# Turning K in place on VectorE instead of through TensorE, in a one-core decode attention kernel

## The chip, the cores and the metric

The kernel runs on one core of a Trainium2 chip. The metric is the device time of one execution in microseconds, as a median of runs. A profile is one further execution, recorded instruction by instruction.

## The reference

One decoding step for 8 batches: layer norm of `x`, attention over the last W = 2048 keys of a cache, and a gated unit that multiplies the attention's output.

```
xn = layernorm(x)                                   # x: (8, 1, 512)
q  = (xn @ wq)  as 32 query heads of 128            # wq: 512 x 4096
k, v = last 2048 keys of k_cache, v_cache           # (8, 8 heads, 8192, 128), bf16; 4 query heads share one
o  = softmax(q k^T / sqrt(128)) v
s  = o @ wo                                         # wo: 4096 x 512
g  = silu((sigmoid(xn @ w_gate) * (xn @ w_up)) @ w_down)   # 512 -> 1792 -> 512
out = x + s * g
```

The inputs that must be read are 33.6 MB of K, 33.6 MB of V, 4.2 MB each of `wq` and `wo`, and 5.5 MB of the gated unit's weights, 81.0 MB in all.

## The kernel before

**Loads.** All big inputs pass through one ring of 9 SBUF buffers of 16 KB per partition (`RING`), 2 MB for a K or V load. SyncE's queue (SP) issues them in one fixed order, `issue_loads`: the two halves of `wq` (`wq_sb`), then K and V loads merged by slot (K load i at slot 4i, V load i at slot 4i + `PV_LAG`, here 11), with the three matrices of the gated unit (`wg_sb`, `wu_sb`, `wd_sb`) ahead of the last two V loads, and `wo` in eight pieces at the end. There are 16 K loads and 16 V loads. A load is issued when its turn has come and a buffer is free; a K buffer is free after its last slot, a V buffer likewise. A K or V load holds one batch and 4 of the 8 KV heads: 128 partitions are 32 groups of keys times 4 heads (head innermost), each with 64 keys in a row, 16 KB that lie together in HBM.

**Slots.** A K load is worked off in 4 slots, so there are 64 slots; `manual_schedule` keeps the written order on each engine. In slot t the loop calls `k_half(t, 0)` and `k_half(t, 1)`: 4 TensorE transposes each (L415) of 128 x 128 32-bit words (two bf16 of the head dimension are one word) into the PSUM tile `kT_ps`, and a VectorE copy (L419) into `kT_sb` that also sorts the columns by head. Every second slot `qk` does 8 score matmuls of 512 columns (L434) into `s_ps`; their four 32-column groups of the array are the four heads of the load, and successive matmuls go to different groups.

**Softmax.** One batch at a time, over 8 slots: the maximum on VectorE (`soft_max_part`, L446), a small fp32 matmul that joins the maxima (`soft_exp`, L455), Exp on ScalarE (L460), a VectorE 32 x 32 block transpose of the probabilities (`soft_turn`, L474), one matmul with a permutation (`soft_permute`, L480), a ScalarE copy (L488), and four VectorE products with a head mask (`soft_mask`, L496). The denominators are L507, L518 and L520.

**Values and the end.** `pv(u)`, 11 slots behind, does 8 matmuls of 256 columns (L536) per slot on four column groups; after four slots ScalarE copies `acc_ps` out (L549) and `pv_sum` sums it (L557, L564). The gated unit (L307 to L344) runs once, eight slots before the end of `pv`, and waits for its weights. After the last V load come `pv`, `pv_sum`, `o_rows` (L579, L588), then 64 matmuls with `wo` (L647), two VectorE products (L658, L660) and the store of the output.

Of the kernel before, what the change touches and what calls it, by code (L numbers as in the profile page):

```python
# [10 lines left out]
def kernel(  # L11
# [14 lines left out]
    P = 128  # L26
# [13 lines left out]

    GL = 4
# [5 lines left out]
    HALF = CC // 2  # L47
    NX = NG * NJ
    XR = NX * rep
    NT = B * NG  # L50
    SPB = NG * NJ
    NSLOT = B * SPB
    PV_LAG = SPB + 3

    D2 = Dh // 2
    NJ2 = NJ // 2
    QB = 2 * rep
    QPAD = XR - QB
    RING = 9
# [15 lines left out]
    ktpool = ctx.enter_context(tc.tile_pool(name="ktpool", bufs=2))  # L75
    ppool = ctx.enter_context(tc.tile_pool(name="ppool", bufs=2))
    psum = ctx.enter_context(
# [31 lines left out]
    def load_kv(cache, i, name):  # L109
        b, gg = divmod(i, NG)  # L110
        t = ring_tile([P, CH, Dh], name)
        load(
            t[:].rearrange("p c d -> p (c d)"),
            cache[b, GL * gg : GL * (gg + 1), win0:Sk, :].rearrange(
                "j (p c) d -> p j (c d)", c=CH
            ),
        )
        return t
# [26 lines left out]
    loads += [(3, 0), (3, 1)]  # L145
    loads_done = [0]
    free_bufs = [RING - 2]
# [15 lines left out]
    def issue_loads():  # L163
        while loads_done[0] < len(loads) and free_bufs[0] > 0:
            kind, i = loads[loads_done[0]]
            if kind == 0:
                k_tiles[i] = load_kv(A_k_cache, i, "k_sb")
            elif kind == 1:
                v_tiles[i] = load_kv(A_v_cache, i, "v_sb")
            elif kind == 2:  # L170
                load_mlp(i)
            else:
                load_wo(i)
            loads_done[0] += 1
            free_bufs[0] -= 1
# [10 lines left out]

    ident = consts.tile([P, P], bf16, name="ident")
    make_identity(nc, ident[:])
    identf = consts.tile([P, P], f32, name="identf")
    make_identity(nc, identf[:])  # L190
    SumM = consts.tile([P, P], f32, name="SumM")
    nc.gpsimd.memset(SumM[:], 0.0)
    for off in range(-rep * (NJ - 1), rep * NJ, rep):
        nc.gpsimd.affine_select(  # L194
            out=SumM[:],
            in_=SumM[:],
            compare_op=ALU.not_equal,
            fill=1.0,
            base=-off,
            pattern=[[-1, P]],  # L200
            channel_multiplier=1,
        )
    BS = rep * NJ
    SumM_blk = SumM[:].rearrange("p (a i) -> p a i", i=BS)
    nc.gpsimd.affine_select(
        out=SumM_blk,
        in_=SumM_blk,
        compare_op=ALU.is_ge,
        fill=0.0,
        base=0,  # L210
        pattern=[[-BS, P // BS], [0, BS]],
        channel_multiplier=1,
    )
    nc.gpsimd.affine_select(
        out=SumM_blk,
        in_=SumM_blk,
        compare_op=ALU.is_ge,
        fill=0.0,
        base=BS - 1,
        pattern=[[BS, P // BS], [0, BS]],  # L220
        channel_multiplier=-1,
    )
# [3 lines left out]
    Jneg = consts.tile([P, NJ], f32, name="Jneg")  # L226
    nc.vector.tensor_reduce(
        out=Jneg[:],
        in_=ident[:].rearrange("p (a j r) -> p j a r", j=NJ, r=rep),
        axis=AX.XY,  # L230
        op=ALU.add,
    )
    nc.vector.tensor_scalar(
        out=Jneg[:], in0=Jneg[:], scalar1=-scale, scalar2=None, op0=ALU.mult
    )

# [6 lines left out]
    )  # L243

# [6 lines left out]
    )  # L251

    perm = consts.tile([P, P], bf16, name="perm")
    nc.vector.tensor_copy(
        out=perm[:].rearrange("k (p gl) -> k p gl", gl=GL),
        in_=ident[:].rearrange("k (gl p) -> k p gl", gl=GL),
    )

    QW = 3 * QPAD + 2 * QB
    qz_sb = work.tile([P, B, Hkv, QW], bf16, name="qz_sb")
# [25 lines left out]
    xnT_ps = psum1.tile([P, KT, B], bf16, name="xnT_ps", tag="pT_ps")  # L288
# [14 lines left out]
    def unit_in(w_sb):  # L303
        d_ps = psum.tile([P, FQ], f32, name="d_ps", tag="kT_ps")
# [43 lines left out]
    def q_projection():  # L348
        HH = Hq // 2
        q_ps = [  # L350
            psum.tile([P, HH, 32], f32, name=f"q_ps{hh}", tag="kT_ps") for hh in range(2)
        ]
        for kt in range(KT):
            for hh in range(2):
                for c in range(4):
                    nc.tensor.matmul(  # L356
                        q_ps[hh][32 * c : 32 * (c + 1), :, :],
                        lhsT=xnT_sb[:, kt, :],
                        rhs=wq_sb[kt // KH][:, kt % KH, :].rearrange(
                            "p (h a m e) -> p h a m e", a=2, m=32, e=2  # L360
                        )[:, HH * hh : HH * (hh + 1), c % 2, :, c // 2],
                        start=(kt == 0),
                        stop=(kt == KT - 1),
                        tile_position=(0, 32 * c),
                        skip_group_check=True,
                    )
        for hh in range(2):
            q_sb = ppool.tile([P, HH * 32], bf16, name="q_sb", tag="p_bf")
            nc.scalar.copy(out=q_sb[:], in_=q_ps[hh][:].rearrange("p h m -> p (h m)"))
            qT_sb = ppool.tile([P, HH * 32], bf16, name="qT_sb", tag="pt_bf")  # L370
            nc.vector.transpose(out=qT_sb[:], in_=q_sb[:])  # L371
            GH = Hkv // 2
            for e in range(2):
                for c2 in range(2):
                    for r in range(rep):
                        nc.vector.tensor_copy(  # L376
                            out=qz_sb[
# [24 lines left out]

    CP = CC // 2
    HP = CP // 2

    def k_half(t, h2):
# [287 lines left out]
```

## Time and profile before

| | |
|---|---|
| median of 3 runs | 199.43 us (199.40 to 199.49) |
| profiled execution: time, span | 199.47 us, 197.7 us |
| mean granted TensorE clock | 0.904 |
| PE, DVE, ACT, POOL busy | 146.0, 125.2, 22.9, 9.0 us |
| read from HBM | 81.02 MB, 410 GB/s over the span |

The span runs from the first to the last instruction; the profiled execution's own time is 1.8 us longer. PE is TensorE's matmuls, PEld its weight loads, DVE is VectorE, ACT is ScalarE, POOL is GpSimd, SPq is SyncE's queue that issues loads. A group of instructions is told by its line (L419), and its columns are the busy time in all, the mean duration of one in ns, and the idle time just before them with what ended it.

### The profile page before, as it was taken

Reading aid. Unit: us, or ns where it says so; the run is one execution under the profiler, and the core shown is the slowest. Engines: PE = TensorE matmul, PEld = TensorE weight load, DVE = VectorE, ACT = ScalarE, POOL = GpSimd, SP = SyncE. Lnnn points to the kernel's source line nnn. Section 1 sums busy time; section 2 is a strip of 40 time slices with the busy share of each in tenths; the row PEclk is TensorE's granted clock in tenths of the full one; section 3 lists DMA queues with packets and bytes.
Section 4 is the critical chain, followed back from the end, with each engine's and each line's share of the span. In section 5 each row is a group of like instructions: output and inputs, shape, how many; then the busy total and the mean of one; then the engine's idle time right before and its main releaser. Section 6 shows DMA issues by size and latency. Waiting matters only on the chain.

```text
span 197.7 us, 3707 instructions
## 1 busy us (share of the span) xinstructions
PE 146.0 (74%) x1576; PEld 101.4 (51%) x1576; DVE 125.2 (63%) x280; ACT 22.9 (12%) x48; POOL 9.0 (5%) x22
## 2 busy tenths in 40 slices
PE   0073598939996997998697969686929697747693
PEld 0023455626765675665565756465626565325582
DVE  2809877964787887868765777577807786143111
ACT  2001000130011003002100110030000300600000
POOL 7910000000000000000000000000000000000000
PEclk9999999995999999999979699999975999697558
DMA  6999999999999999999999999999999999999980
GB/s 220 423 434 444 434 434 416 428 428 434 431 434 431 424 431 424 424 434 434 434 428 423 431 424 434 434 431 428 428 424 434 424 442 423 434 426 409 419 324 21
DMA packets 6864, 81.26 MB, mean 411 GB/s; under 512 B 792, under 2 KB 1088, under 8 KB 2112
## 3 DMA queue, kind: packets, MB, share of 16 engines
q1 hardware_dynamic: 6752, 81.01, 96.5%
q8 instruction: 12, 0.20, 0.4%
q14 instruction: 4, 0.03, 0.0%
q10 hardware_dynamic: 32, 0.01, 0.0%
q0 software_dynamic: 64, 0.01, 0.0%
HBM read 81.02 MB, written 0.01 MB: 410 GB/s over the span
## 4 chain that ended last, share of the span: by engine, by line
DMA 53%; PE 33%; DVE 10%; ACT 2%; issue 1%; SPq 0%; ACTq 0%
DMA k_sb<-in_A_k_cache_dram 32%; PE kT_ps L415 17%; DMA v_sb<-in_A_v_cache_dram 15%; DMA wq_sb<-in_A_wq_dram 6%; PE s_ps L434 5%; PE acc_ps L536 4%; DVE kT_sb L419 4%; PE a_ps L647 3%; DVE qz_sb L376 2%; DVE pT_sb L496 1%; PE oT_ps L557 1%; PE q_ps L356 1%; DVE qT_sb L371 1%; DVE pt_bf L474 1%; ACT L460 1%
## 5 line engine op out<-in xcount | busy, mean ns | idle before, releaser
L419 DVE COPY kT_sb<-kT_ps 128x512 f32<-128x512 f32 x128 | 83.7, 686 | 34.0 <-PE kT_ps L415 32.0
L415 PE MATMUL kT_ps<-identf,k_sb 128*128 128x128 f32 x512 | 78.8, 300 | 15.3 <-DMA k_sb<-in_A_k_cache_dram 11.6
L415 PEld LDWEIGHTS kT_ps<-identf,k_sb 128*128 128x128 f32 x512 | 62.1, 153 | 38.0 <-issue 20.7
L536 PE MATMUL acc_ps<-v_sb,pT_sb 128*32 128x256 bf16 x512 | 27.0, 299 | 9.7 <-DVE pT_sb L496 7.6
L536 PEld LDWEIGHTS <-pT_sb 128*32 128x32 bf16 x512 | 11.7, 101 | 19.7 <-DVE pT_sb L496 9.0
L434 PE MATMUL s_ps<-kT_sb,qz_sb 128*32 128x512 bf16 x256 | 21.5, 413 | 0.3 <-DVE kT_sb L419 0.3
L549 ACT COPY acc_sb<-acc_ps 128x256 f32<-128x256 f32 x16 | 6.0, 372 | 70.9 <-PE acc_ps L536 70.9
L460 ACT ACTIVATE p_bf<-s_ps,nm 128x512 bf16<-128x512 f32 x8 | 5.5, 687 | 46.3 <-DVE nm L457 46.3
L557 PE MATMUL oT_ps<-Sel,acc_sb 128*128 128x16 f32 x64 | 9.4, 261 | 2.0 <-ACT acc_sb L549 1.1
L557 PEld LDWEIGHTS oT_ps<-Sel,acc_sb 128*128 128x128 f32 x64 | 9.2, 208 | 3.2 <-ACT acc_sb L549 2.0
L496 DVE TENSOR_SCALAR pT_sb<-pc_bf,Hm 128x512 bf16<-128x512 bf16 x32 | 9.1, 346 | 0.0
L480 PE MATMUL pT_ps<-pt_bf,perm 128*128 128x512 bf16 x8 | 3.2, 402 | 7.4 <-DVE pt_bf L474 7.4
L290 PE MATMUL xnT_ps<-ident,xn_bf 8*128 8x8 bf16 x4 | 0.3, 174 | 9.6 <-DVE xn_bf L280 9.6
L434 PEld LDWEIGHTS <-qz_sb 128*32 128x32 bf16 x256 | 4.0, 96 | 6.1 <-issue 6.1
L474 DVE STREAM_TRANSPOSE pt_bf<-p_bf 128x512 bf16<-128x512 bf16 x8 | 5.6, 704 | 1.7 <-ACT p_bf L460 1.7
L647 PE MATMUL a_ps<-wo_sb,o_sb 128*32 128x256 bf16 x64 | 6.3, 388 | 0.0
L446 DVE TENSOR_REDUCE mx<-s_ps 128x1 f32<-128x512 f32 x8 | 5.5, 685 | 0.9 <-PE s_ps L434 0.9
L520 DVE RECIPROCAL rden<-den_ps 128x32 f32<-128x32 f32 x8 | 2.9, 358 | 5.1 <-PE den_ps L518 5.1
L647 PEld LDWEIGHTS <-o_sb 128*32 128x32 bf16 x64 | 5.4, 138 | 0.7
L488 ACT CAST pc_bf<-pT_ps 128x512 bf16<-128x512 f32 x8 | 4.7, 586 | 6.4 <-PE pT_ps L480 6.4
L194 POOL TENSOR_SCALAR_AFFINE_SELECT SumM<-SumM 128x128 f32<-128x128 f32 x7 | 5.4, 770 | 0.5
L564 DVE TENSOR_TENSOR oT_sb<-oT_ps,rden 128x16 bf16<-128x16 f32 x16 | 2.7, 166 | 4.2 <-PE oT_ps L557 4.2
(63 smaller groups left out, 60.5 us busy)
## 6 DMA issues: line engine op xcount, KB each, us to landing
k_sb<-in_A_k_cache_dram SPq DMA_DIRECT2D x16, 2048.0 KB, 31.4
v_sb<-in_A_v_cache_dram SPq DMA_DIRECT2D x16, 2048.0 KB, 35.5
wq_sb<-in_A_wq_dram SPq DMA_DIRECT2D x2, 2048.0 KB, 9.6
wo_sb<-in_A_wo_dram SPq DMA_DIRECT2D x2, 1024.0 KB
wg_sb<-in_B_w_gate_dram SPq DMA_DIRECT2D x1, 1792.0 KB, 34.0
wu_sb<-in_B_w_up_dram SPq DMA_DIRECT2D x1, 1792.0 KB, 36.3
wd_sb<-in_B_w_down_dram SPq DMA_DIRECT2D x1, 1792.0 KB, 32.9
wo_sb<-in_A_wo_dram SPq DMA_DIRECT2D x3, 512.0 KB, 24.1
```

The lines of the kernel that those rows point to most:

```text
L194: nc.gpsimd.affine_select(out=SumM[:], in_=SumM[:], compare_op=ALU.not_equal, fill=1.0, base=-off, pattern=[[-1, P]], channel_multiplier=1,)
L415: nc.tensor.transpose(out=kT_ps[:, uu, :], in_=kw[:, u0 + uu, :], identity=identf[:, :])
L419: nc.vector.tensor_copy(out=kT_tiles[t // 2][:, o0 : o0 + HP, :, :], in_=kT_ps[:].rearrange("p u (k gl) -> p u gl k", gl=GL),)
L434: nc.tensor.matmul(s_tiles[b][XR * gl : XR * (gl + 1), :], lhsT=qz_sb[:, b, GL * gg + gl, z0 : z0 + XR], rhs=kT[:, :, gl, :, e], start=(x ...
L446: nc.vector.reduce_max(out=mx[:], in_=s_tiles[b][:], axis=AX.X)
L460: nc.scalar.activation(out=p_bf[:], in_=s_tiles.pop(b)[:], func=AF.Exp, bias=nm[:], scale=scale, accum_out=den128[:],)
L474: nc.vector.transpose(out=pt_bf[:], in_=p_bf[:])
L496: nc.vector.tensor_scalar(out=pT_tiles[b][:, :, gl, :], in0=pc, scalar1=Hm[:, gl : gl + 1], scalar2=None, op0=ALU.mult,)
L536: nc.tensor.matmul(acc_tiles[i][32 * c : 32 * (c + 1), :], lhsT=pT_tiles[b][:, x * (CC // 2) + n, :, :].rearrange("p g n -> p (g n)"), rhs ...
L549: nc.scalar.copy(out=acc_sb[:], in_=acc_tiles.pop(i)[:])
L557: nc.tensor.matmul(oT_ps[:], lhsT=acc_sb[:, Dh * c2 : Dh * (c2 + 1)], rhs=Sel[:].rearrange("p (g c r) -> p c g r", g=GL, c=2)[:, c2], star ...
L647: nc.tensor.matmul(a_ps[32 * c : 32 * (c + 1), :], lhsT=o2_sb[:, hg, j, :], rhs=wo_parts[hg, j][:, DC * c : DC * (c + 1)], start=(n == 0), ...
```

## The change

- A K load now holds 16 KV heads (both batches of a pair) and a quarter of their keys: 128 partitions are 16 heads times 8 groups of keys, each again with 64 keys in a row (16 KB). Size and number of the K loads stay; V loads are as before.
- `k_turn(t)`: VectorE transposes a quarter of the load in place, 32 x 32 blocks of 32-bit words, [128 x 1024] words per slot. The TensorE transposes, `kT_ps` and `kT_sb` are gone.
- `qk(i, gl)` reads the turned K with steps: 4 matmuls of 512 columns per slot, 16 per K load, 256 in all as before. All 16 of one load write the same 32-column group (the load's quarter of the keys); The 128 partitions of the turned K are four blocks of 32 words, one block for each four heads, and `qz_sb` holds a query only in its own block, with zeros in the others.
- Softmax for two batches at a time, every 16 slots: two tiles of scores, Exp twice, two block transposes (`soft_turn`), then `soft_spread`: 8 matmuls of 512 columns per pair, half of them masked out of PSUM by one VectorE product each, half by four ScalarE copies each.
- `PV_LAG` is 26 slots, so seven K loads go ahead of the first V load; the ring has 10 buffers, and a buffer is matched to the load ten places earlier. The gated unit keeps its place against `pv`.
- Some constants that GpSimd built come from VectorE; the 32 small copies into `qz_sb` become 16.

```diff
-    PV_LAG = SPB + 3
-    RING = 9
+    PV_LAG = SPP + 10
+    RING = 10
...
+    def load_k(i):
+        pr, tq = divmod(i, NTQ)
+        k0 = win0 + tq * KP * CH
+        t = ring_tile([P, CH, Dh], "k_sb")
+        load(
+            t[:].rearrange("p c d -> p (c d)"),
+            A_k_cache.rearrange("b h s d -> (b h) s d")[
+                2 * Hkv * pr : 2 * Hkv * (pr + 1), k0 : k0 + KP * CH, :
+            ].rearrange("h (k c) d -> h k (c d)", c=CH),
+        )
+        return t
...
-        for uu in range(HP):
-            nc.tensor.transpose(
-                out=kT_ps[:, uu, :], in_=kw[:, u0 + uu, :], identity=identf[:, :]
-            )
-        nc.vector.tensor_copy(
-            out=kT_tiles[t // 2][:, o0 : o0 + HP, :, :],
-            in_=kT_ps[:].rearrange("p u (k gl) -> p u gl k", gl=GL),
-        )
+    def k_turn(t):
+        i, j = divmod(t, NJ)
+        kw = (
+            k_tiles[i][:, CC * j : CC * (j + 1), :]
+            .rearrange("p c d -> p (c d)")
+            .bitcast(f32)
+        )
+        nc.vector.transpose(out=kw, in_=kw)
...
+    def qk(i, gl):
+        pr, tq = divmod(i, NTQ)
+        u, gl2 = divmod(gl, 2)
+        if tq == 0 and gl2 == 0:
+            s_tiles[pr, u] = psum3.tile([P, CH * KP], f32, name="s_ps")
+        kT = k_tiles[i][:].rearrange("p c (a g k e) -> p c a g k e", a=NA, g=GL, e=2)
+        for a in range(NA):
+            for e in range(2):
                 nc.tensor.matmul(
+                    s_tiles[pr, u][32 * tq : 32 * (tq + 1), :],
+                    lhsT=qz_sb[:, pr, gl, 2 * a + e, :],
+                    rhs=kT[:, :, a, gl, :, e],
+                    tile_position=(0, 32 * tq),
...
+    def soft_spread(pr, c4, half):
+        ch, c2 = divmod(c4, 2)
+        c0 = CBH * half
+        pT_ps = psum.tile([P, CBH, NQ * GL, rep], f32, name="pT_ps")
         nc.tensor.matmul(
+            pT_ps[:].rearrange("p c g r -> p (c g r)"),
+            lhsT=spread[:, c4, :],
+            rhs=pt_tiles[pr][:, c0 : c0 + CBH].rearrange("p c q u n -> p (c q u n)"),
             start=True,
             stop=True,
         )
+        out = pT_tiles[pr][:, c0 : c0 + CBH, ch, :, c2, :]
+        if c2 == 0:
+            nc.vector.tensor_tensor(
+                out=out,
+                in0=pT_ps[:],
+                in1=Hx[:].rearrange("p (c q) g r -> p c (q g) r", q=NQ),
+                op=ALU.mult,
+            )
+        else:
+            for gl in range(GL):
+                nc.scalar.activation(
+                    out=out[:, :, gl::GL, :],
+                    in_=pT_ps[:, :, gl::GL, :],
+                    func=AF.Copy,
+                    scale=Hm[:, gl : gl + 1],
+                )
...
         if t < NSLOT:
-            k_half(t, 1)
+            k_turn(t)
...
-        if 0 < t <= NSLOT and t % 2 == 0:
-            qk(t // 2 - 1)
+        if NJ <= t < NSLOT + NJ:
+            qk(t // NJ - 1, t % NJ)
```

## The prediction

> **What bounds the kernel now.** I read the engines' busy times first, then the DMA parts, then the chain that ended last, and last the windows of half a microsecond at the end.
>
> ```profile
> PE 146.0 (74%) x1576; PEld 101.4 (51%) x1576; DVE 125.2 (63%) x280; ACT 22.9 (12%) x48; POOL 9.0 (5%) x22
> ...
> q1 hardware_dynamic: 6752, 81.01, 96.5%
> q8 instruction: 12, 0.20, 0.4%
> ...
> DMA 53%; PE 33%; DVE 10%; ACT 2%; issue 1%; SPq 0%; ACTq 0%
> ...
> k_sb<-in_A_k_cache_dram SPq DMA_DIRECT2D x16, 2048.0 KB, 31.4
> ```
>
> No compute engine is busy over 74% of the span, but the queue q1, which carries all the loads, keeps the 16 DMA engines busy for 96.5% of 197.7 us, 190.8 us. A load is issued 31.4 us before it lands, and 2.10 MB at the usual 429 GB/s take 4.9 us, so more than six loads always wait in the queue. The third of the chain that runs over PE is therefore mostly work that keeps pace with the loads. The end shows it:
>
> ```profile
> 191.00:191.50 0.50, 0.50 (x9) 0.44 (x6) 0.00 (x0) 0.00 (x0) 0.00 (x0) 0.50 0.54 211
> 192.50:193.00 0.50, 0.50 (x9) 0.44 (x6) 0.00 (x0) 0.00 (x0) 0.00 (x0) 0.50 0.27 102
> 193.50:194.00 0.50, 0.50 (x12) 0.46 (x9) 0.00 (x0) 0.00 (x0) 0.00 (x0) 0.78 0.11 39
> 194.00:194.50 0.50, 0.50 (x12) 0.36 (x6) 0.00 (x0) 0.00 (x0) 0.00 (x0) 1.00 0.00 0
> ```
>
> The last three columns are TensorE's clock, the DMA engines' busy share and GB/s. By 191.0 us half of the engines are through; the last run until 194. So the engines finish some 3 us apart, and a load counts as landed only with its slowest engine. Behind that stands a fixed tail:
>
> ```profile
> 154.94 29.30 DMA v_sb<-in_A_v_cache_dram
> ...
> 188.48 6.11 PE a_ps L647 x63
> ...
> 194.62 0.42 DVE prod L658
> ```
>
> The last V load lands at 184.2, and 10.4 us later, at 194.6, the matmuls with wo end, at half clock; the store ends the span 3.1 us after that. The last piece of wo lands at about 194, so both ways give the same end.
>
> **The change, part by part.** All sums go against the profiled 199.47 us (span 197.7, 1.8 outside), 0.04 above the median. A measurement here tells about 0.2%, 0.4 us, from no change.
>
> ```profile
> L419 DVE COPY kT_sb<-kT_ps 128x512 f32<-128x512 f32 x128 | 83.7, 686 | 34.0 <-PE kT_ps L415 32.0
> L415 PE MATMUL kT_ps<-identf,k_sb 128*128 128x128 f32 x512 | 78.8, 300 | 15.3 <-DMA k_sb<-in_A_k_cache_dram 11.6
> L434 PE MATMUL s_ps<-kT_sb,qz_sb 128*32 128x512 bf16 x256 | 21.5, 413 | 0.3 <-DVE kT_sb L419 0.3
> L474 DVE STREAM_TRANSPOSE pt_bf<-p_bf 128x512 bf16<-128x512 bf16 x8 | 5.6, 704 | 1.7 <-ACT p_bf L460 1.7
> L325 DVE STREAM_TRANSPOSE hT_sb<-h_sb 128x448 bf16<-128x448 bf16 x1 | 1.0, 979 | 0.0
> ```
>
> *VectorE.* Gone: 83.7 us of copies (L419), 9.1 of mask products (L496), half of the copies into qz_sb (2.2). Added: 64 turns of 1024 words. No row shows a transpose of 32-bit words. The contiguous row (L474) gives 704 ns for 512 elements; the maximum (L446) has 685 for 512 and short VectorE instructions 0.15 to 0.2 us, so I take 0.17 us fixed and 1.04 ns an element: 0.17 + 1.07 = 1.24 us. The row with steps (L325) has 1.80 ns an element: 2.0 us; two passes over each word would be 2.3. I take 1.24, as the turn is contiguous on both sides: 64 x 1.24 = 79 us. The 16 products out of PSUM are 0.69 us each (L323: 622 ns for 448), 11 us. Sum: 125.2 - 83.7 - 9.1 - 2.2 + 79 + 11 = 120 us. Per pair of batches: 16 turns 19.8, products 2.8, maxima 1.4, block transposes 1.4, small ones about 2.2: 27.6 us, while the pair's eight loads take 39.1. So 11.5 us per pair remain.
>
> *TensorE.* Gone: 78.8 us. The scores lose their neighbours: before, four column groups ran side by side, 8 matmuls in 0.55 us in the chain, which is 0.27 us for each alone. Now one load's 16 go to one group. Bounds: 84 ns (21.5/256, still side by side) and 0.40 us (L480's whole duration); I take 0.27, 69 us in place of 21.5. Per pair: scores 17.3, pv 6.8 (27.0/4), sums 2.4, spread 8 x 0.40 = 3.2, joins and denominators 0.9: 30.6 of 39.1.
>
> *ScalarE.* 64 masked copies of 128 elements in place of 8 casts (4.7 us); L549 has 372 ns for 256, so at most 64 x 0.37 = 24 us, 42 in all, far from a bound. *GpSimd* and constants: their work ends before the second half of wq (13.0 us); nothing.
>
> *Loads and queues.* Bytes and the 16 KB rows stay. k_turn waits for its K load at the head of VectorE's slot; behind it wait maxima and products, hence pv and the release of buffers. What covers it is the ring: a load needs the buffer of ten loads before, so a buffer has nine loads, 44 us, from its load's landing to its next issue, and K needs 5.0 us of turning, 4.3 of scores and a wait for about two V loads in PE's order, some 20 us. SP holds no other work. If that cover were gone, each late release would leave all 16 engines idle. At the start seven K loads arrive 4.9 us apart against 5.0 of turning, from about 19 us on: a lag of one load, paid from the same cover. V's tail is the old one.
>
> *Instruction fetch.* q8 moves 12 packets of 16 KB for 3152 matmuls and weight loads, one per some 260. The change takes 1024 away with the transposes, adds 48 for the spread and takes 32 from joins and denominators: 2144, so 8 packets. A packet holds an engine 0.4% x 16 x 197.7 / 12 = 1.05 us, as long as 1.7 rows of 16 KB. Spread evenly, 12 packets could not put engines 3 us apart, so some engines must have served two or three. Four packets fewer are worth 4 x 1.05/16 = 0.3 us if spread evenly, 2.1 if the slowest engine loses two; I take one packet and a little, 1.2 us, since 8 of 12 of the 3 us leaves 2.0. The last V load and the last piece of wo both land that much earlier, and the tail follows, whether at half clock or waiting for wo. [...]
>
> Sum: 199.47 - 1.2 = 198.3 us.
>
> **The rivals.**
>
> *Nothing gained (0.13).* The late engines are late for another reason (small rows of wo), or the lost packets were others'. For: the trace does not name engines. Time 199.4.
>
> *K rows far apart (0.17, slower).* Before, the rows of four heads 2 MB apart (8192 x 256 B) alternate while a key group steps 16 KB; now eight rows of a head follow each other and 16 heads lie 2 MB apart, so if each engine takes one head, all 16 read at the same place in 2 MB. Against: the old order has 2 MB steps between neighbouring rows and runs at 429 GB/s. K is 33.55 MB, 78.2 us; from 1.5% less rate the gain is gone. The slowest streaming window of 5 us has 406 GB/s, 5.7% less: +4.4, 202.7 us. [...]
>
> *VectorE becomes the bound (0.10, slower).* If a turn takes 2.0 us (the L325 rate), a pair takes 39.8, and the last softmax ends at 19 + 159 = 178. Behind it: pv of four loads 9, the gated unit 8 (171 to 179 in the trace), output rows and wo 10, end 3: 208, with 1.8 outside 210 us. It decides from about 1.85 us; two passes give 229.
>
> *TensorE runs cold (0.10, slower).* PE waits between bursts, and the windows show a clock of 0.50 to 0.59 after such waits (45 to 50 us, 145 to 150 us). 30.6 us per pair include a clock of 0.904, so 27.7/c; with 23 us ahead and 24 behind it decides from c = 0.73; c = 0.70 gives 207 us. Against: at 45 to 50 us PE was busy throughout and by 50 to 55 us the clock was back at 0.96, so the backlog mends itself.
>
> **How the numbers follow.** Forecast 0.50, nothing gained 0.13, the three slower ones 0.37. The low end takes the 2.1 us: 197.3. The high end, 206, takes in K's 202.7 with room; left out are VectorE (0.10) and about half of TensorE's and a quarter of K's (0.09). The forecast's own range is 197.3 to 199.2.
>
> **What would show it.** Right: turns of 1.24 us, 8 packets on q8, full DMA share to the end, the last V load at about 183 and engines at most 2 us apart. Wrong: K packets that move less than 429 GB/s while K is loading; turns of 1.85 us and more; a DMA share below 0.9 in mid-span, which would mean late buffers; or 8 packets and an end at 194 all the same.

## The result: 302.1 us, half as long again

The changed kernel takes 302.13 us (median; 296.57 to 302.39) against 199.42 us before in the same session. Two further executions took 300.20 and 304.73 us. The ratio is 1.496, with a 95% interval of 1.481 to 1.512. The executions fall into a faster group (here 296.57 and 300.20 us) and a slower one (here 301.91 to 304.73), and ratios here and below are taken over the faster one, so that a ratio can lie under that of the medians. The prediction was 198.3 us with a range to 206.0, so it was wrong in sign and size.

The profile after is of an execution of 296.57 us with a span of 294.8 us. First the page: engines, slices, queues and the chain that ended last.

```profile
PE 147.8 (50%) x1072; PEld 71.1 (24%) x1072; DVE 117.1 (40%) x188; ACT 35.7 (12%) x104; POOL 2.3 (1%) x10
...
GB/s 287 387 213 217 213 213 213 216 218 211 218 347 213 353 213 331 213 342 207 320 200 271 249 216 292 213 289 207 253 229 220 349 427 434 426 427 429 417 300 21
...
q1 hardware_dynamic: 6752, 81.01, 96.9%
q8 instruction: 8, 0.13, 0.2%
...
another core or an unknown queue 34%; DMA 29%; DVE 18%; PE 14%; issue 2%; SPq 1%; ACT 1%; DVEq 0%; ACTq 0%
...
k_sb<-in_A_k_cache_dram SPq DMA_DIRECT2D x16, 2048.0 KB, 66.0
```

VectorE and ScalarE work no longer than forecast. TensorE's scores do, 84.3 us (L420, below) for 69, at a granted clock of 0.72; it is idle for half of the span all the same. The queue q1 moves the same 6752 packets and 81.01 MB and is again busy for 97% of the span, but the span is half as long again. So the same bytes cost the DMA engines 1.5 times the time. The GB/s row (slices of 7.4 us) shows where: 213 from the third slice on, while K alone is loading; 200 to 353 once V loads come in between; and 426 to 434 in the five slices from 236 us on, after the last K load. Before the change the same row, in slices of 4.9 us, has no such stretch:

```profile
GB/s 220 423 434 444 434 434 416 428 428 434 431 434 431 424 431 424 424 434 434 434 428 423 431 424 434 434 431 428 428 424 434 424 442 423 434 426 409 419 324 21
```

Second, the groups of the turn, the scores and the values, and the longest wait:

```profile
L409 DVE STREAM_TRANSPOSE k_sb<-k_sb 128x1024 f32<-128x1024 f32 x64 | 76.0, 1220 | 104.9 <-DMA k_sb<-in_A_k_cache_dram 104.9
L420 PE MATMUL s_ps<-k_sb,qz_sb 128*32 128x512 bf16 x256 | 84.3, 495 | 36.0 <-DVE k_sb L409 31.6
L543 PE MATMUL acc_ps<-v_sb,pT_sb 128*32 128x256 bf16 x512 | 53.4, 365 | 58.4 <-DMA v_sb<-in_A_v_cache_dram 58.0
```

A turn takes 1.22 us, as forecast, and VectorE sits idle for 104.9 us in front of the turns, all of it for K loads. TensorE waits for VectorE, and for V loads.

Third, two windows of 5 us, one with K alone in flight and one after the last K load. The last three columns are TensorE's clock, the busy share of the 16 DMA engines and GB/s:

```profile
30.00:35.00 5.00, 2.78 (x12) 1.06 (x11) 1.84 (x2) 0.00 (x0) 0.00 (x0) 1.00 1.00 213
245.00:250.00 5.00, 2.63 (x42) 1.52 (x41) 3.04 (x8) 1.71 (x5) 0.00 (x0) 1.00 1.00 429
```

This is the whole result in two lines. In both windows the DMA engines are busy without a gap, yet with K they move 213 GB/s, to within a per cent half of 429. At 429 GB/s an engine takes 16,384 / 26.8e9 s = 0.61 us for a row of 16 KB, at 213 GB/s 1.23 us. The factor is two to within a per cent, with the engines busy throughout; where the second 0.61 us goes, no window shows.

### The profile page after: what moved, and what is told of

Its sections match the earlier page's. It is cut to its first block, busy times and chain, and to the rows that moved or that the text cites. A ratio compares the mean times of both kernels' runs of the same rounds, so it can differ in the third digit from the quotient of the medians.

```text
span 294.8 us, 2619 instructions
## 1 busy us (share of the span) xinstructions
PE 147.8 (50%) x1072; PEld 71.1 (24%) x1072; DVE 117.1 (40%) x188; ACT 35.7 (12%) x104; POOL 2.3 (1%) x10
## 3 DMA queue, kind: packets, MB, share of 16 engines
q1 hardware_dynamic: 6752, 81.01, 96.9%
## 4 chain that ended last, share of the span: by engine, by line
another core or an unknown queue 34%; DMA 29%; DVE 18%; PE 14%; issue 2%; SPq 1%; ACT 1%; DVEq 0%; ACTq 0%
DMA k_sb<-in_A_k_cache_dram 17%; DVE k_sb L409 14%; DMA v_sb<-in_A_v_cache_dram 13%; PE s_ps L420 6%; PE acc_ps L543 2%; PE a_ps L651 2%; DVE pT_sb L492 2%; PE oT_ps L564 2%; PE pT_ps L483 1%; DVE mx L434 1%; SPq L95 1%; DVE mj L437 0%; ACT p_bf L455 0%; PE o_ps L586 0%
## 5 line engine op out<-in xcount | busy, mean ns | idle before, releaser
L409 DVE STREAM_TRANSPOSE k_sb<-k_sb 128x1024 f32<-128x1024 f32 x64 | 76.0, 1220 | 104.9 <-DMA k_sb<-in_A_k_cache_dram 104.9
L420 PE MATMUL s_ps<-k_sb,qz_sb 128*32 128x512 bf16 x256 | 84.3, 495 | 36.0 <-DVE k_sb L409 31.6
L543 PE MATMUL acc_ps<-v_sb,pT_sb 128*32 128x256 bf16 x512 | 53.4, 365 | 58.4 <-DMA v_sb<-in_A_v_cache_dram 58.0
L420 PEld LDWEIGHTS <-qz_sb 128*32 128x32 bf16 x256 | 27.7, 117 | 84.9 <-issue 67.5
L543 PEld LDWEIGHTS <-pT_sb 128*32 128x32 bf16 x512 | 23.3, 110 | 70.2 <-issue 62.9
L500 ACT ACTIVATE pT_sb<-pT_ps,Hm 128x128 bf16<-128x128 f32 x64 | 18.3, 368 | 46.4 <-PE pT_ps L483 46.4
L492 DVE TENSOR_TENSOR pT_sb<-pT_ps,Hx 128x512 bf16<-128x512 f32 x16 | 10.8, 674 | 18.8 <-PE pT_ps L483 18.8
L483 PE MATMUL pT_ps<-pt_bf,spread 128*128 128x512 bf16 x32 | 13.3, 487 | 7.5 <-DVE pT_sb L492 7.2
L564 PE MATMUL oT_ps<-Sel,acc_sb 128*128 128x16 f32 x64 | 13.5, 329 | 4.2 <-ACT acc_sb L556 3.2
L360 PE MATMUL q_ps<-wq_sb,xnT_sb 128*32 128x512 bf16 x32 | 3.8, 627 | 1.5 <-DMA wq_sb<-in_A_wq_dram 1.3
```

The lines of the kernel that those rows point to most:

```text
L409: nc.vector.transpose(out=kw, in_=kw)
L420: nc.tensor.matmul(s_tiles[pr, u][32 * tq : 32 * (tq + 1), :], lhsT=qz_sb[:, pr, gl, 2 * a + e, :], rhs=kT[:, :, a, gl, :, e], start=(gl2 ...
L483: nc.tensor.matmul(pT_ps[:].rearrange("p c g r -> p (c g r)"), lhsT=spread[:, c4, :], rhs=pt_tiles[pr][:, c0 : c0 + CBH].rearrange("p c q ...
L492: nc.vector.tensor_tensor(out=out, in0=pT_ps[:], in1=Hx[:].rearrange("p (c q) g r -> p c (q g) r", q=NQ), op=ALU.mult,)
L500: nc.scalar.activation(out=out[:, :, gl::GL, :], in_=pT_ps[:, :, gl::GL, :], func=AF.Copy, scale=Hm[:, gl : gl + 1],)
L543: nc.tensor.matmul(acc_tiles[i][32 * c : 32 * (c + 1), :], lhsT=pT[:, (CC // 2) * j + n, 32 * Q : 32 * (Q + 1)], rhs=v_sb[:, CC * j + 2 * ...
```

## The experiments

Two theories stood against each other at first. *Distance* (A in the expectations): 16 heads 2 MiB apart are slow to read out of HBM, the prediction's rival. *The turn* (B): VectorE's turn in place slows the loads. A third came up after the pitch sweep below, *dealing*: the rate goes with the outer count of the access pattern, which is 16 in the new one (16 heads of 8 rows) and was 32 in the old one (32 groups of 4 rows). The outer count is the size of the slowest dimension that the load's source is written with. The name is the author's guess that this count settles which DMA engine gets which rows; no trace names the engine of a row.

### Is it the K loads alone?

`k_old_rows` is the changed kernel with one edit:

```diff
-            A_k_cache.rearrange("b h s d -> (b h) s d")[
-                2 * Hkv * pr : 2 * Hkv * (pr + 1), k0 : k0 + KP * CH, :
-            ].rearrange("h (k c) d -> h k (c d)", c=CH),
+            A_k_cache[i // NG, GL * (i % NG) : GL * (i % NG + 1), win0:Sk, :].rearrange(
+                "j (p c) d -> p j (c d)", c=CH
+            ),
```

> The changed kernel, but each K load takes the rows of the kernel before (one batch, 4 heads, all 2048 keys, heads alternating from row to row); the compute is unchanged, so the scores are made from rows in the wrong places. Theory A (HBM serves the 16 heads' rows, 2 MiB apart, at half rate): K loads at 429 GB/s again, 8 packets on q8, span about 196.5 us, time 198.3 (0.5% below before). Theory B (VectorE's in-place turn slows the writes of the loads into SBUF, or the reads of TensorE do): still 213 GB/s while K loads, time about 297. Theory C (the half rate is A, but the rest of the lost time, some 19 us, is compute that waits): K at 429 GB/s, time 205 to 220.

It took 198.1 us (198.06 to 198.19), ratio 0.993 (0.992 to 0.995). Its slices, queue and groups, then two windows at the end:

```profile
GB/s 225 432 427 437 429 437 437 427 427 427 427 427 427 430 437 430 427 434 434 434 430 434 425 424 427 427 434 434 427 430 434 430 423 429 424 440 422 405 384 37
...
q8 instruction: 8, 0.13, 0.2%
...
L409 DVE STREAM_TRANSPOSE k_sb<-k_sb 128x1024 f32<-128x1024 f32 x64 | 75.2, 1215 | 16.1 <-DMA k_sb<-in_A_k_cache_dram 16.1
L420 PE MATMUL s_ps<-k_sb,qz_sb 128*32 128x512 bf16 x256 | 71.0, 427 | 19.8 <-DVE k_sb L409 15.2
```

```profile
191.00:191.50 0.50, 0.05 (x2) 0.00 (x0) 0.00 (x0) 0.00 (x0) 0.00 (x0) 1.00 0.61 234
192.50:193.00 0.50, 0.49 (x8) 0.17 (x4) 0.00 (x0) 0.00 (x0) 0.00 (x0) 1.00 0.02 6
```

With the old rows the rate is 422 to 440 GB/s from the second slice until the loads run out, and the time is the predicted one to 0.2 us. So the K pattern carries the whole loss, and the rest of the change does what the prediction said. `before_new_rows` is the reverse, the kernel before with only the K loads' rows of the change, and still its transposes on TensorE:

> The kernel before, with the K loads' rows of the changed kernel alone (16 heads, 512 keys each; TensorE transposes and all compute as before, on rows in the wrong places). A: K loads at about 213 GB/s, 16 x 4.9 = 78 us more at least, time 277 to 300. B: 199.4, unchanged.

It took 315.5 and 326.7 us, longer than the 277 to 300 of theory A, with slices of 203 to 230 GB/s wherever K loads have the most of them. Turning on VectorE has no part in the half rate.

### Distance or dealing

Two kernels changed the distance alone: in the changed kernel each K load's 16 heads are read at a pitch of 2 MiB + 16 KB and of 2 MiB + 1 KB, with the window of the keys moved to make room, so they read other keys.

```diff
+    SKEW = 64        # keys of 256 bytes: 16 KB; 4 in skew_1k
...
+            flat_k[h0 * Sk * Dh + k0 * Dh :][: 2 * Hkv * (Sk + SKEW) * Dh]
+            .rearrange("(h x) -> h x", h=2 * Hkv)[:, : KP * CH * Dh]
+            .rearrange("h (k y) -> h k y", k=KP),
```

> The changed kernel, its 16 heads of one load read 2 MiB + 16 KiB apart instead of 2 MiB (each head starts 64 keys later than the one before; other keys of the same cache, so the scores are of other keys). A: the rows no longer sit at the same place in 2 MiB, K at 429 GB/s, about 198.3 us. A' (it is the number of heads open at once, not the equal low address): still 213 GB/s, about 297. B: about 297.

> As the run with 16 KiB, but 2 MiB + 1 KiB apart (4 keys). A with a coarse interleave in HBM (some KiB): between, 220 to 290 us. A with a fine interleave (1 KiB or less): about 198.3. A' and B: about 297.

They took 309.7 to 314.5 us and 301.1 to 307.2 us: no recovery from either.

`pitch_sweep` has no computation, only loads of 2 MB through eight buffers, six of each kind; a VectorE copy of one column tells when each has landed.

> No attention at all: only loads of 2 MB from the K cache (128 rows of 16 KB), six of each pattern in turn, each followed by a one-column VectorE copy that shows when it has landed; the output is x. The patterns: the old rows (4 heads alternating); 16 blocks of 128 KB that lie 128 KB, 256 KB, 512 KB, 1 MiB, 2 MiB (the change's) and 4 MiB apart; 2 MiB plus 16 KB, 64 KB, 128 KB, 256 KB and 1 MiB apart; 8 heads alternating from row to row; then 2 MiB and 128 KB again. Old rows 4.9 us a load, 2 MiB 9.8 us in every theory. Theory A'' (equal address bits below 2 MiB down to a coarse grain of 64 KB or more): 2 MiB + 128 KB and + 256 KB are back at 4.9 us, + 16 KB is not, and 4 MiB is as slow as 2 MiB. Theory A' (sixteen different 2 MiB regions at once, whatever the offset): every pitch of 2 MiB and more takes 9.8 us, 1 MiB (8 regions) some 5 to 7, and 512 KB and less 4.9; 8 heads alternating 4.9 to 7.

In the timeline of VectorE's copies the first column is the copy's start. The bracket holds VectorE's idle time before it, and that, with the copy's 0.16 us, is the time from one landing to the next:

```profile
42.38 0.16 DVE L81 COPY seen<-p128k 128x1 bf16<-128x1 bf16 x1 [4.75 <-DMA p128k<-in_A_k_cache_dram]
...
81.83 0.16 DVE L81 COPY seen<-p256k 128x1 bf16<-128x1 bf16 x1 [9.68 <-DMA p256k<-in_A_k_cache_dram]
...
666.57 0.16 DVE L81 COPY seen<-eight 128x1 bf16<-128x1 bf16 x1 [9.55 <-DMA eight<-in_A_k_cache_dram]
```

The time per load does not depend on the pitch from 256 KB up: 9.7 to 9.85 us, but for one load of 9.97, at 256 KB, 512 KB, 1, 2 and 4 MiB and at 2 MiB plus 16 KB to 1 MiB. Both forms of the distance theory, A' and A'', missed. At 128 KB it is 4.85 us in five of six loads (5.2 in the last), and there the 16 blocks of 8 rows follow each other without a gap, so that the pattern can be taken as 128 rows in one line; that it was is not shown. `eight`, whose rows go through 8 heads in turn, is slow too; what it has in common with the others is 16 as the outer count.

`deal_sweep` then varied the outer count over bytes that lie together:

```diff
+    def near(n, cnt):
+        """the same 128 rows that follow each other, dealt as cnt x 128/cnt"""
+        ... flat[n * P * ROW : (n + 1) * P * ROW].rearrange("(j b x) -> b j x", b=cnt, x=ROW)
```

> Loads only, 2 MB each. near8 to near128: 128 rows of 16 KB that follow each other in HBM, to the same 128 partitions; only the outer count of the source pattern differs. far16, far32, far64: 16, 32, 64 heads 2 MiB apart, 8, 4, 2 rows of each. [...] Addresses (heads far apart are slow to read): near16 4.85, far32 and far64 9.7. [...] half_1q: 64 rows to the lower 64 partitions, then 64 to the upper, on one queue; half_2q: on two queues at once. row_1q: the rows of far16 by eight loads of one row of each head; row_2q: the same on two queues, partitions 8h to 8h+3 and 8h+4 to 8h+7 under way together. [...] far16_pool: far16 from GpSimd's queue, 9.7 if dealt the same. near8: 9.7 or more.

With the two times of `pitch_sweep`, dealing gives 9.7 us for `near16` and `far16` and 4.85 for `near32` to `near128`, `far32` and `far64`; distance gives 4.85 for all the near kinds and 9.7 for all the far ones.

The kinds `near32`, `near16` and `near64` in this order, one landing of each (the profile leaves the digits out of the names):

```profile
13.33 0.16 DVE L115 COPY seen<-near 128x1 bf16<-128x1 bf16 x1 [4.74 <-DMA near<-in_A_k_cache_dram]
...
52.65 0.16 DVE L115 COPY seen<-near 128x1 bf16<-128x1 bf16 x1 [9.54 <-DMA near<-in_A_k_cache_dram]
...
100.89 0.16 DVE L115 COPY seen<-near 128x1 bf16<-128x1 bf16 x1 [4.67 <-DMA near<-in_A_k_cache_dram]
```

4.9, 9.7 and 4.8 us for the same amount of neighbouring rows to the same 128 partitions. `near128` took 4.8 us, `far16` 9.7 us, and `far32`, twice as many heads 2 MiB apart, 4.8 to 5.9 us with one of 7.3. In the near kinds the order of the rows over the partitions changes with the outer count; the far kinds and the pitch sweep have other orders, and there too 16 is slow and 32 fast. Distance is out as the cause.

Several expectations of this run were missed. `far64` took 7 to 10 us, not the 4.85 of dealing. `near8` took 19 to 37 us; why was not taken apart. `row_2q` took 17 to 21 us in four of six, longer than `row_1q` (8 to 9, the last 26). In both SyncE's queue waited for earlier loads of the same kind (82.2 and 41.2 us in all), so neither tells what the dealing costs. `far16_pool` ran beside `row_2q` and says nothing. `half_1q` began at 9.7 us and drifted up to 14.7; `half_2q` took 4.7 to 10.1. `deal_again` set the unclear kinds apart:

> Loads only, as in the sweep of the dealing, with its unclear kinds apart from each other: far64 with near64 behind it, far32, half_1q (ten each; eight for far64), near128 ahead of half_2q, whose second queue waits until they are done. [...] far64: 4.85 if the 7 to 10 us of before came from its neighbours; 7 to 10 again if 64 heads 2 MiB apart are slow to read by themselves, so that addresses count too.

A landing each of `far64`, `far32` and `half_1q`:

```profile
69.45 0.16 DVE L113 COPY seen<-far 128x1 bf16<-128x1 bf16 x1 [4.67 <-DMA far<-in_A_k_cache_dram]
...
114.11 0.16 DVE L113 COPY seen<-far 128x1 bf16<-128x1 bf16 x1 [4.69 <-DMA far<-in_A_k_cache_dram]
...
183.50 0.16 DVE L113 COPY seen<-half_1q 128x1 bf16<-128x1 bf16 x1 [9.27 <-DMA half_1q<-in_A_k_cache_dram]
```

`far64` now takes 4.8 to 6.0 us, so most of its slowness came from its neighbours in the first sweep; up to 1.2 us a load stay unexplained. `far32` takes 4.85 in nine of ten; the tenth, with `half_1q` behind it, takes 7.4. `half_1q` has the outer count 64 and bytes that lie together, but fills 64 partitions at a time, and takes 8.8 to 9.4 us in nine of ten (the last 11.2), so that a high outer count alone does not give 4.85. Nor do two queues that fill the two halves at once: `half_2q` takes 8.2 to 9.7 us after a first one of 16.7.

What is shown: the half rate goes with the outer count of 16, at every pitch from 256 KB to 4 MiB (9.7 to 9.97 us) and over rows that follow each other (`near16`, 9.5 to 9.7), and also with a destination of 64 partitions at a time (8.8 to 9.4). Why is not shown: no trace here names the engine that moves a row, or what it waits for.

Last, the same test inside the changed kernel. K load i takes the 2 MB of head 4i, which lie together, dealt as 16 times 8 or as 32 times 4:

```diff
+            A_k_cache.rearrange("b h s d -> (b h) (s d)")[4 * i, :].rearrange(
+                "(j b x) -> b j x", b=16, x=CH * Dh      # b=32 in k_near32
+            ),
```

> The changed kernel, but K load i takes 128 rows of 16 KB that follow each other in HBM (the 2 MB of head 4i, not the keys of the window), dealt as 16 times 8: nothing lies apart any more, the outer count is still 16. Dealing: 295 to 305 us as the changed kernel, 213 GB/s where K alone is loading. Addresses: 198.1 us.

> The same 2 MB for each K load, dealt as 32 times 4. Both theories: 198.1 us, 429 GB/s throughout; with k_near16 it changes the outer count alone. If the rows that follow each other cost something of their own, this shows it.

305.1 us (301.6 to 306.8), ratio 1.524 (1.517 to 1.531), and 198.16 us (198.07 to 198.22), ratio 0.9935 (0.992 to 0.995). The window from 30 to 35 us of `k_near16`:

```profile
30.00:35.00 5.00, 3.52 (x11) 1.19 (x10) 1.84 (x2) 0.00 (x0) 0.00 (x0) 1.00 1.01 216
```

and of `k_near32`:

```profile
30.00:35.00 5.00, 4.28 (x25) 1.74 (x23) 5.00 (x5) 0.00 (x0) 0.00 (x0) 1.00 1.02 436
```

One number in a `rearrange`, 16 or 32, over the same bytes, is worth 107 us. That the outer count of 16 costs the half rate is settled; by what mechanism is not.

### Where the 1.3 us of `k_old_rows` come from

The prediction's only gain was four instruction packets fewer. Three kernels put instructions back where nothing waits for them: `k_old_rows` with GpSimd memsets in each of the 90 slots, 12 of 64 words, 24 of 8 words, or 7 of 8 words.

```diff
+        for _ in range(12):        # 24 in fill24, 7 in fill7
+            nc.gpsimd.memset(filler[:], 0.0)
```

> The changed kernel with the old K rows (198.1 us) and 1080 small memsets on GpSimd, which otherwise has nothing to do; nothing waits for them. They bring the instructions back to about the number of the kernel before, so 12 packets on q8 in place of 8. Theory of instruction fetch (each packet holds a DMA engine for about 1 us, and the engine that serves most of them ends last): 199.3 us if the added packets fall as those of the kernel before, at least 198.4 (4 x 1.05 / 16 = 0.3 more) if they are spread evenly. Rival (the 1.3 us come from the order of the loads and the longer ring, not from fetch): 198.1, no change.

> The same with 2160 memsets, 16 or 17 packets on q8. Fetch: about 200.5 us if each four packets cost 1.2, at least 198.7 if spread evenly. Rival: 198.1.

> The changed kernel with the old K rows (198.1 us) and 630 memsets on GpSimd, few enough to be through (some 100 us) before the loads are. In fill12 and fill24 GpSimd itself ended the span, but the last product came 2.25 and 3.83 us later than without memsets, with 10 and 17 more instruction packets on q14 of 8 KB each, 0.22 us for each. Fetch: 5 or 6 more packets, 199.2 to 199.5 us. Rival (the delay there came from GpSimd running beside the end): 198.1.

The first two were badly sized. GpSimd took 0.105 to 0.152 us for a memset and about 0.06 us between two, and so ended the span itself, at 232.4 and 357.2 us. Their packets did not come on q8 either, but on q14, in pieces of 8 KB:

```profile
q14 instruction: 21, 0.17, 0.1%
q8 instruction: 8, 0.13, 0.1%
```

(`fill24`; `k_old_rows` has 4 on q14.) These counts are of the whole span, and `fill12` and `fill24` go on fetching after the loads are through. What can be compared is the start of the last VectorE product, which needs the last piece of wo, and the packets up to it:

| kernel | 8 KB packets on q14 before the last product | last product starts | later than in `k_old_rows`, us | us for each packet more |
|---|---|---|---|---|
| `k_old_rows` | 3 | 193.74 | | |
| `fill7` | 8 | 194.74 | 1.00 | 0.20 |
| `fill12` | 10 | 195.99 | 2.25 | 0.32 |
| `fill24` | 12 | 197.57 | 3.83 | 0.43 |

The end moves with the packets, but a packet has no fixed price. The 0.22 us that the expectation of `fill7` works with counts packets that came too late to matter, so that this forecast was met in part by luck. Nor do the packets' own times add up to the delay: the nine more of `fill24` take 2.9 us together in its trace. How the delay comes about can be seen at the end of the loads, first in `k_old_rows`, then twice in `fill24`:

```profile
193.00:194.00 1.00, 0.25 (x2) 0.06 (x1) 0.68 (x2) 0.00 (x0) 0.00 (x0) 1.00 0.00 0
```

```profile
193.00:194.00 1.00, 1.00 (x19) 0.97 (x16) 0.00 (x0) 0.00 (x0) 0.62 (x6) 0.84 0.06 25
195.00:196.00 1.00, 0.50 (x8) 0.42 (x8) 0.00 (x0) 0.00 (x0) 0.65 (x7) 1.00 0.06 23
```

A DMA share of 0.06 is one engine of 16. After 193 us `k_old_rows` has no load under way, while in `fill24` a single engine still moves 23 to 25 GB/s: one engine ends late, as the prediction had it. That this engine is the one that served the packets is inferred, since the traces do not name engines.

`fill7`, whose memsets end in time, took 199.21 us (199.01 to 199.57), 1.1 us more than `k_old_rows` and as expected, and is as slow as the kernel before (ratio 0.9993, 0.998 to 1.000). 630 instructions on an idle engine, for which nobody waits, cost nearly as much as the change had won. That the change's own 1.3 us are its four packets alone fits this but is not shown, since the order of the loads changed too. The longer ring is out: `four_key_mixed`, below, has 9 buffers again, 8 packets on q8 and 198.43 us.

### A load that is dealt well and holds its own data

`k_old_rows` and `k_near32` read keys into places where the scores take them for others. Six steps led to a kernel that is fast with its own data. All load K with the old rows.

`four_key_blocks` adapts the rest: after the turn the four blocks of 32 partitions are quarters of the keys of four heads, and a score matmul has 128 columns of queries, with zeros outside their block.

```diff
-        kT = k_tiles[i][:].rearrange("p c (a g k e) -> p c a g k e", a=NA, g=GL, e=2)
+        kT = k_tiles[i][:].rearrange("p c (a k g e) -> p c a k g e", a=NA, g=GL, e=2)
...
-                    rhs=kT[:, :, a, gl, :, e],
+                    rhs=kT[:, :, a, :, gl, e],
```

> The changed kernel with K loaded as before (one batch, four heads, 32 groups of keys; outer count 32) and everything else adapted to it: VectorE turns it in place, the four blocks of 32 partitions are then four quarters of the keys, and each score matmul has 128 columns of queries with zeros outside their block (four tiles of queries, filled by 8 ScalarE copies per load); ring of 9 buffers in place of 10. Theory of the dealing and the prediction's other steps: 198.1 us, as the run with the old rows, ratio 0.993 (0.990 to 0.996); DMA at 429 GB/s throughout; ScalarE 36 + 128 copies of some 0.2 to 0.3 us, 60 to 75 us, off the path. If the ninth and tenth buffers matter, or the copies delay the scores, 199 to 201 us. If a transposed K costs the loads anything by itself, over 203.

332.7 to 341.1 us, far from the 198.1 expected. The groups of the turn and the scores:

```profile
L449 PE MATMUL s_ps<-k_sb,qz_sb 128*128 128x512 bf16 x256 | 227.4, 1033 | 8.0 <-DVE k_sb L438 5.8
L438 DVE STREAM_TRANSPOSE k_sb<-k_sb 128x1024 f32<-128x1024 f32 x64 | 74.8, 1213 | 0.0
```

A score matmul takes 1033 ns, where `k_old_rows` has 376 at best. The four heads are now interleaved word by word, so TensorE reads one word out of every 16 bytes. `four_key_sorted` lets the turn write the words of a head side by side:

```diff
-        nc.vector.transpose(out=kw, in_=kw)
+        nc.vector.transpose(
+            out=kw.rearrange("p (b g k) -> p b k g", g=GL, k=KP),
+            in_=kw.rearrange("p (b k g) -> p b k g", g=GL, k=KP),
+        )
```

> four_key_blocks, but the turn writes the words of a head side by side within each block of 32 (8 keys, then the next head), so that a score matmul reads 8 neighbouring words as in the changed kernel, not one word of each 16 bytes. Theory (the 1034 ns of a score matmul come from the 16-byte step of its moving operand, and only K's loads were wrong in the change): score matmuls back at 376 ns where four_key_blocks has 1034, DMA at 429 GB/s to the end, 198.1 us, ratio 0.993, if the turn keeps its 1.22 us; VectorE's bound as the prediction has it if a turn with steps takes 2.0 us: some 210. Rival (the matmul is slow because it has 128 columns of queries in place of 32): 1034 ns again and 330 to 341 us.

```profile
L438 DVE STREAM_TRANSPOSE k_sb<-k_sb 128x1024 f32<-128x1024 f32 x64 | 119.6, 1966 | 0.0
L452 PE MATMUL s_ps<-k_sb,qz_sb 128*128 128x512 bf16 x256 | 78.0, 443 | 37.7 <-DVE k_sb L438 29.1
```

211.0 us (210.1 to 211.1), ratio 1.057 (1.056 to 1.059). The matmuls are back at their old price with 128 columns of queries, so it was the step. Now the turn takes 1.97 us, and the time is what the prediction's rival "VectorE becomes the bound" gave for turns of 2.0 us, 210. `four_key_act` gave VectorE's masked products to ScalarE:

```diff
-        if c2 == 0:
-            nc.vector.tensor_tensor(out=out, in0=pT_ps[:], in1=Hx[:]..., op=ALU.mult)
-        else:
             for gl in range(GL):
                 nc.scalar.activation(...)
```

> four_key_sorted with VectorE's 16 masked products (0.69 us each, 11 us) given to ScalarE, as the other half of them already is (four copies of 0.37 us each). VectorE per pair of batches: 16 turns of 1.97 us and 5 us of small ones, 36.5 us, under the 39.1 us that the pair's loads take; ScalarE 57 + 23 = 80 us in all. If VectorE's rate was all that held four_key_sorted up: 198 to 200 us, faster than the kernel before if the fetch gain of 1.3 us is kept. If what is late is TensorE behind VectorE (it waits for each turn, then for ScalarE's copies): 202 to 207 us.

204.5 us (202.1 to 208.9), ratio 1.017 (1.014 to 1.021): the second forecast, though VectorE is down from 161.4 to 149.8 us and DMA runs at the full rate until 190 us (407 to 443 GB/s in each slice from 5 us on). `four_key_early` shortened VectorE's chain:

```diff
             nc.vector.transpose(out=qT_sb[:], in_=q_sb[:])
+            k_turn(gg)        # the turns of slots 0 and 1
...
-            nc.vector.tensor_scalar(out=dh[:, u, :], ...)
+            nc.scalar.activation(out=dh[:, u, :], in_=Sel[:], func=AF.Copy, scale=den128[:, u : u + 1])
```

> four_key_act with the first two turns put between the steps of the queries (VectorE sat idle there; the first turn came at 23 us, the first K load some 4 us before), and the 8 products for the denominators (0.34 us each) given to ScalarE. VectorE's last turn at about 150 us in place of 157, so the last softmax some 6 us earlier. If that chain sets four_key_act's end (its loads are through at 190 us, at full rate): 198 to 200 us. If TensorE's own work after it does: 202 to 205 us, no change.

202.1 us (200.9 to 206.2), ratio 1.011 (1.010 to 1.013). VectorE's last turn ended at 154 us, 3 us earlier and not 7, and the time fell by less still. Some of the chain that ended last in `four_key_early`, in order of time, tells what is late:

```profile
152.13 1.86 DVE k_sb L359
...
164.35 4.25 ACT pT_sb L515 x16
...
171.07 2.19 ACT pT_sb L515 x8
...
191.96 5.01 PE a_ps L664 x63
```

VectorE's last turn, then ScalarE's masked copies of the last pair of batches, then all of TensorE's tail; no DMA is in it. `four_key_pairs` asked what the steps themselves cost, with pairs of heads side by side:

```diff
-            out=kw.rearrange("p (b g k) -> p b k g", g=GL, k=KP),
+            out=kw.rearrange("p (b g k h) -> p b k g h", g=2, k=KP, h=2),
...
-                    rhs=kT[:, :, a, gl, :, e],
+                    rhs=kT[:, :, a, gl // 2, :, gl % 2, e],
```

> four_key_early with words sorted half as far: the turn writes pairs of heads side by side (2 neighbouring words, then a step), and a score matmul reads every second word (8-byte step). It separates the price of the step in VectorE's writes from that in TensorE's reads. If a turn's price goes with the length of the run that it writes: 1.22 to 1.6 us a turn in place of 1.96; if any step costs the same, 1.96. If TensorE pays 2 ns for each 16 bytes that it touches (1034 ns / 512 with one word each): 1034 / 2 = 517 ns a score matmul; if every step over 4 bytes costs the same, 1034. With 1.4 and 517: 198 to 200 us; with 1.96 and 517 (36 us more on TensorE): 203 to 212; with 1034, over 300.

```profile
L444 PE MATMUL s_ps<-k_sb,qz_sb 128*128 128x512 bf16 x256 | 117.7, 605 | 6.7 <-ACT qz_sb L415 3.5
L359 DVE STREAM_TRANSPOSE k_sb<-k_sb 128x1024 f32<-128x1024 f32 x64 | 74.2, 1210 | 0.0
```

212.5 us (211.2 to 216.3). Writing runs of two words costs VectorE nothing, 1.21 us; the matmul at an 8-byte step takes 605 ns (587 at least), above the 517 expected, and TensorE becomes the bound. `four_key_mixed` buys each price where there is room: every fourth K load by pairs, the rest sorted, and the last pair's masked products half on VectorE again.

```diff
+    def pairs(i):
+        return 2 if i % NQ == 1 else 1
...
+            out=kw.rearrange("p (b g k h) -> p b k g h", g=GL // G2, k=KP, h=G2),
+            in_=kw.rearrange("p (b k g h) -> p b k g h", g=GL // G2, k=KP, h=G2),
...
+        if pr == NPAIR - 1 and c2 == 0:
+            nc.vector.tensor_tensor(out=out, in0=pT_ps[:], in1=Hx[:]..., op=ALU.mult)
+            return
```

> four_key_early with every fourth K load turned by pairs (1.21 us a turn and 607 ns a score matmul, as four_key_pairs has them) and the other twelve fully sorted (1.97 us and 376 to 430 ns), and with half of the last pair's masked products back on VectorE, which is idle by then (0.69 us in place of four ScalarE copies of 0.41). VectorE 16 x 0.76 = 12 us less, TensorE some 13 us more. If VectorE's lag at the last softmax and ScalarE's copies behind it (173 us at the end of the last ones, 24 us ahead of the last product) set four_key_early's end: 198 to 199.5 us, and the loads set it again. If TensorE's added work is late in its place: 201 to 204.

```profile
PE 139.6 (71%) x1076; PEld 59.8 (30%) x1080; DVE 141.7 (72%) x167; ACT 70.8 (36%) x288; POOL 8.6 (4%) x16
...
q1 hardware_dynamic: 6752, 81.01, 97.2%
q8 instruction: 8, 0.13, 0.2%
...
L372 DVE STREAM_TRANSPOSE k_sb<-k_sb 128x1024 f32<-128x1024 f32 x64 | 107.4, 1778 | 0.2 <-DMA k_sb<-in_A_k_cache_dram 0.2
L460 PE MATMUL s_ps<-k_sb,qz_sb 128*128 128x512 bf16 x256 | 81.6, 456 | 20.3 <-DVE k_sb L372 8.6
```

198.43 us (198.41 to 198.55), ratio 0.995 (0.994 to 0.996): faster than the kernel before by 0.5%, and than the change by a third. VectorE and TensorE are both near 140 us. The chain that ended last closes with the loads of wd and wo (26% of the span), so the queue sets the end again.

## Why the prediction was wrong

**The step that failed** is the first sentence of its part on loads and queues: "Bytes and the 16 KB rows stay." Bytes and rows did stay, in size and number. The sentence was taken to mean that the loads keep 429 GB/s, and the GB/s row shows 213 for K. The price is 9.7 to 9.8 - 4.85 = 4.9 us for each of 16 K loads, 78 of the 103 us. The remaining 25 us were not taken apart. Part of them lies where K and V loads alternate: slices 12 to 32 have a mean of 263 GB/s, where one load at 213 and one at 429 make 4.19 MB / 14.6 us = 287. By this estimate some 13 us of those 155 us are lost beyond the half rate.

**The rival "K rows far apart"** looked at the right place, named the right sign of it in the trace (K packets under 429 GB/s while K is loading) and had the wrong mechanism and 3.3 of the 103 us: 202.7, priced by the slowest streaming window. Its argument against, that the old order too has steps of 2 MB, was right about distance. The pitch sweep shows no effect of a pitch of 256 KB to 4 MiB on these reads (9.7 to 9.97 us). What the prediction did not ask is whether a load keeps its rate when its pattern changes from 32 times 4 to 16 times 8, although it wrote down "if each engine takes one head".

**The other terms held**, as `k_old_rows` and the profile after show:

- VectorE: 1.22 us a turn for 1.24, 117 us in all for 120; L325's 1.80 ns an element, 2.0 us a turn, came back as the price of steps, 1.97 us, in `four_key_sorted`.
- TensorE's scores: 71.0 us for 69 in `k_old_rows` (84.3 in the changed kernel, at its lower clock).
- ScalarE: 35.7 us, under the 42 given as a bound. The masked copies took 0.37 us each.
- The ring's cover: no slice of `k_old_rows` but the first and the last few is under 420 GB/s, so no buffer was late.
- Instruction fetch: 8 packets, and engines that end 1.5 to 2 us apart (a share of 0.61 at 191.0 us and 0.02 at 192.5) for the kernel before's 3. The term of 1.2 us measured 1.3. It was a guess between 0.3 and 2.1, and the fill runs give no fixed price of a packet, so that the close match is in part luck.
- TensorE running cold: its clock in `k_old_rows` was lower, 0.85 for 0.90, and cost nothing while the loads set the pace.

## What to carry to other kernels

Read a load's rate from the trace per pattern, as the GB/s of a window with that load alone at a DMA share of 1.00: a full share says that the engines are occupied, not that they move what they can (213 and 429 GB/s here, both at 1.00). When a change reorders a load's source pattern, price the new outer count as a new kind of load, and try it with loads alone before anything is built on it; here 32 kept the rate (4.85 us for 2 MB) and 16 halved it (9.7 us). A data layout that suits the loads may not suit its readers: the order that kept the rate cost TensorE or VectorE their fast steps (605 or 1033 ns a score matmul for 376, or 1.97 us a turn for 1.22), and the kernel won only once each price was paid on the engine with room.

## What the runs showed of the hardware

- 128 rows of 16 KB to 128 partitions load in about 4.85 us (most loads) with an outer count of 32 and, where the rows follow each other, of 64 or 128 as well; 64 blocks 2 MiB apart take 4.8 to 6.0 us (`deal_sweep`, `deal_again`). With an outer count of 16 they take 9.5 to 9.97 us, whether the rows follow each other (`near16`) or blocks of them lie 256 KB to 4 MiB apart (`pitch_sweep`); 16 blocks 128 KB apart, which leave no gap, take 4.85. 64 partitions at a time take 8.8 to 9.4 us in nine of ten loads for the same 2 MB (`half_1q` in `deal_again`).
- A matmul of 512 columns takes 378 ns (median) with its moving elements 4 bytes apart (`k_old_rows`), 607 at 8 bytes (`four_key_pairs`) and 1034 at 16 bytes (`four_key_blocks`).
- VectorE's transpose of 1024 words takes 1.22 us in place (`k_old_rows`), 1.21 us when it writes runs of two words (`four_key_pairs`), and 1.97 us when it writes single words 32 bytes apart (`four_key_sorted`).
- 630, 1080 and 2160 memsets on an otherwise idle GpSimd (`fill7`, `fill12`, `fill24`) brought 5, 7 and 9 more instruction packets of 8 KB ahead of the end of the loads, and with them the last product came 1.0, 2.25 and 3.83 us later, in a kernel that is bound by its loads.
